# Turned placement for the inversion of two batches, and a new written order of all engines

## The chip, the cores and the metric

The kernel runs on one core of a Trainium2 chip. The metric is the device time of one execution in microseconds (us). The core's engines run side by side, each in the order of its own queue: TensorE (PE) multiplies matrices, VectorE (DVE), ScalarE (ACT) and GpSimd (POOL) work element by element, and SyncE (SP) issues the transfers (DMA). PE writes into PSUM, which has eight banks; the others read it there (not POOL) and keep their data in SBUF.

## The reference

Three stages, each fed by the one before. First a Nystrom attention for 4 batches of 8 heads, 576 positions and 64 features; then a layer with a cosine; then one with a leaky rectifier. q, k, v and alpha are float32, the weights of the layers 64-bit.

```
q_lm, k_lm = means over groups of 18 positions (32 landmarks)
A  = softmax(q k_lm^T / 8)      576 x 32
Bm = softmax(q_lm k_lm^T / 8)    32 x 32
C  = softmax(q_lm k^T / 8)       32 x 576
Z  = Bm^T / (norm1(Bm) * norminf(Bm) + 1e-6)
for 6 times:  Z = 2 Z - Z Bm Z
x  = A Z C v                          2304 x 512
h  = x w_in;  x = (h cos h) w_out     512 -> 2048 -> 512
h  = x w_in;  x = (max(h,0) + alpha min(h,0)) w_out
```

The iteration on Z is the inversion that the change is about: 32 matrices of 32x32, 8 in each batch.

## The kernel before, in words

**Storage and names.** A matrix product in full precision is made from rounded halves (high and low), three products for one. `acc`, `h` and `x` are rings of 4, 2 and 2 PSUM banks. All SBUF buffers lie in a few large tiles, so the profile shows nearly all of them as `m`.

**Units of work.** The code makes a list of operations, each with a name `unit:number`. `c` converts a block of 64-bit weights with three DVE steps (lines 575, 577, 579); `u0`, `u1` (batch 0) and `U2` to `U7` load q, k and v of half a batch, make landmarks, softmaxes and the products with v; `z0`, `z1`, `z2` are the inversions of batch 0, of batch 1, and of 2 and 3 together (`z_path`, line 888); `v` and `V` multiply the result with w_in of the first layer into V' (line 1059, casts at 1064 and 1066). `t0` to `t127` are ticks, a block of 128 hidden features for 288 positions: first product (1103), cosine on ACT and DVE (1108 to 1113), rounding (1115), subtraction for the low half (414, on POOL or DVE), second product into `acc` (1128). `b` are the blocks of the third stage, `s`, `y`, `o` and `x` units prepare its operands, `e` stores sums of the second. `w` are fillers (line 540): matmuls without a use, ten at the start and one behind each group of batch 0's inversion.

**Order.** Nothing is scheduled at run time. `ORDER` is one long list of the names; `Plan.go` issues the operations in that order, so each engine's queue is its part of the list. An operation that two engines can do goes to the first in its own list, or, with `/V`, `/A` or `/G` behind the name, to DVE, ACT or POOL. The engines wait for each other by semaphores.

**The inversion of batches 0 and 1 before.** Heads sit as 2 x 4: index i (2), and quadrant qd of 32 partitions (4). The operand of a head is Y = Z Bm (32 columns) beside Z C v (64 columns). A step (`mul`, line 958) multiplies, for each head, Y with both, 8 matmuls of 32x32 by 96, each in two instructions, from partitions of quadrant qd to partitions of the same quadrant of one bank. Then one DVE instruction (line 1006) makes 2 o - product. Five such steps, a last product for the 64 columns (line 1018 behind it), a product with Bm (`wm`, line 1025), and two copies of the result.

**The inversion of batches 2 and 3 before.** With 16 heads the step is another: `residue` (line 977, DVE) makes 2 I - Y once; then `turned` (line 985) multiplies with that, and sends heads of odd i to the neighbouring quadrant (qd xor 1) of a second bank; after six turns each is back. For each of the two banks DVE makes the next residue and ACT or DVE copies the product (`copy`, lines 409 and 411).

Of the kernel before, what the change touches and what calls it, by code (L numbers as in the profile page):

```python
# [13 lines left out]
ALU = mybir.AluOpType  # L14
# [6 lines left out]
u0:1 w:10 u0:2 w:4 c0:1 u1:1 w:2 w:3 u1:2 w:5 u0:4 c1:1 u0:18 c2:1 c9:1 u0:11 u0:5 u0:19 u1:3 c0:2 u0:6/V u0:7 u0:21/A  # L21
u0:20 w:7 c0:3 u0:12 u0:9 c0:4 u0:13 u1:18 u0:8 u0:10 u1:4 u0:22 c3:1 u1:19 u0:23 w:6 u1:20/A u0:3 c1:2 u1:21/A u0:14
c1:3 u1:9 u0:15 u1:7 c1:4 z0:1 u1:8 w:9 z0:2 u1:10 z0:3 c2:2 u0:24 c2:3 u1:5 c9:2 w:8 u0:25 u0:16 z0:4 u1:6 c2:4 w:1
U2:1 u0:17 c9:3 u1:22 u1:11 z0:5 u1:24 z0:6 z0:7 u0:26 z0:8 u0:28 u1:23 u1:12 u0:27 z0:9 c10:1 u1:16 u1:25 u1:13 u1:14
z0:10 c11:1 u1:26 u1:17 z0:11 u0:37 z0:12 u1:28 c9:4 U2:2 u1:27 c3:2 u1:15 u0:29 u0:38 u1:31 c3:3 u1:29 u0:30 u0:31
u0:39 u1:37 c4:1 u1:30 z0:13 u1:34 U3:1 z0:14 u1:32 u0:40 u0:32 u1:33 u0:34 u1:35 c3:4 u0:41 u0:33 u0:35 u1:36 u1:38
u1:39 c5:1 z0:17 u1:40 u0:42 w:11 U2:4 z0:15 u0:36 u1:41 z0:16 z0:18 u0:43 w:12 z0:20 c10:2 u1:42 w:13 z0:21 U2:5 u0:44
c10:3 z0:22 U2:6 u0:45 w:14 z0:23 u0:46 u1:43 z0:24 U2:13 z0:25 c11:2 z0:19 c10:4 z0:26 c11:3 c8:1 U2:14 z0:27 U3:2
u1:44 c11:4 z0:28 U2:16/A u1:45 c4:2 w:15 u1:46 z0:29 u0:47 z0:30 c6:1 w:16 z0:31 u0:48 c4:3 z0:32 U2:15/A u1:47 w:17
z0:33/A z0:34/A v0:1 u0:49/V u1:48 c4:4 v0:2 u1:49 c7:1 v0:4 v0:3 v0:5 U2:10 t0:1 c5:2 U2:12 U2:11 c5:3 U2:7 t0:2 U2:8  # L30
t0:3 t1:1 c8:2 c8:3 U3:13 c5:4 t0:4 c8:4 U3:14 t1:2 U2:9 c8:5 t1:3 c6:2 c12:1 t1:4 t0:5 U3:16/A U3:3 c6:3 U3:15/A t0:6
z1:1 c4:5 t1:5 t0:7 U2:19 z1:2 c5:5 z1:3 c4:6 U2:17 U2:32 t2:1 c2:5 U2:18 c5:6 c14:1 z1:4 U2:20 t1:6 t0:11 U2:21 U2:3
t2:2 U2:31 t0:8 U2:23 t2:3 t1:7 U2:22 t3:1 U2:33 c7:2 t0:10 z1:5 c6:4 v1:1 t2:4 z1:6 c7:3 c10:5 c6:5 t0:9 z1:7 c1:5 z1:8
v1:2 t1:8 t2:5 c6:6 c13:1 t1:11 v1:4 v1:3 t1:9 t2:6 v1:5 t1:10 t3:2 t2:7 t4:1 t3:3 z1:9 t3:4 c7:4 U2:24 t4:2 t3:5 c15:1
t2:8 U2:25 t4:3 t5:1 U2:26/V t4:4 z1:10 c12:2 t3:6 U3:4 t4:5 t5:2 U2:28 t3:7/V t4:6 t6:1 z1:11 c7:5 U2:29 t4:7 t5:3 U3:6
U3:5/V t2:9 c7:6 t6:2 t5:4 U3:7 t6:3 t5:5 t6:4 t2:11 c12:3 U3:8 t8:1 t6:5 U3:9 c14:2 t5:6 t7:1 c12:4 t8:2 t5:7 z1:12
c20:1 U3:10 t8:3 t2:10 t7:2 U3:12/V U3:11 U2:34 t7:3 t8:4 U2:27 z1:13 t6:6 t8:5 t7:4 U2:30 t6:7/V U3:17 t7:5 c14:3 U3:19
z1:14 U3:18 U2:35 t3:9 U3:20 t3:8 U3:21 U2:36 t3:11 U3:22 t3:10 U3:23 U3:31 c13:2 U3:24 z1:15 c13:3 t10:1 U3:25 U2:37
z1:16 U3:28 U3:32 U3:26 z1:17 c14:4 t10:2 U3:27 c13:4 c19:1 t9:1 U3:29 c3:5 c12:5 z1:18 U3:30 U2:38 c0:5 c13:5 c12:6/V
z1:20 c17:1 t9:2 U2:39 c14:5 z1:21 c9:5 t4:8 U3:33 t7:6 z1:22 c13:6 t4:10 z1:23 t10:3 t4:9 U2:40 z1:24 U3:34 t4:11 z1:25  # L40
# [36 lines left out]
U5:29 t50:4 t49:5 U4:35 t50:5 e47:6 e47:7 U6:14 U6:12 t47:8 U6:27 t49:6 t50:6 t49:7 t50:7 U6:13 U6:15 e47:2 U6:16 U5:24
# [272 lines left out]
def kernel(  # L350
# [537 lines left out]
    def z_path(bs, tz):  # L888
# [102 lines left out]
        if b == 2:  # L991
            residue(lambda o=o: o.t[:, :, 0:M], r=[o])
        for it in range(5):
            if b == 2:
                t, pps = zs(f"py{c}", [P, n, W]), [bank(c), bank(c)]
                turned(W, lambda o=o: o.t, [o], pps)
                for x, pp in enumerate(pps):
                    residue(lambda v_=half(pp, W): v_()[:, :, 0:M], slice(x, n, 2), [pp])
# [850 lines left out]
```

## Time and profile before

| | |
|---|---|
| median of the timed runs | 795.76 us (3 runs, 794.31 to 796.95) |
| the profiled execution | 791.91 us |
| its span, first to last instruction | 790.1 us |
| instructions | 18146 |
| PE, weight loads of PE, DVE, ACT, POOL busy | 775.1, 713.9, 637.6, 440.3, 247.5 us |
| granted TensorE clock, mean | 0.999 |

The table's busy times are sums over the span. The profile can cut them into stretches, name for each idle time what ended it, and list the instructions one by one; merged rows say `x` and a count. An instruction's source line can be that of a helper (414 is every subtraction, 409 and 411 every copy).

### The profile page before, as it was taken

The numbers are of one execution on the slowest core, as the hardware profiler recorded it, in microseconds if no ns is written. First come the engines' busy times: TensorE is split into PE (matmuls) and PEld (weight loads), VectorE is DVE, ScalarE is ACT, GpSimd is POOL, SyncE is SP. The second block draws the span as 40 slices with busy tenths as digits, with TensorE's granted clock in tenths as the row PEclk, the third lists the DMA queues.
The fourth block names the chain that finished last, engine by engine and source line by source line (L and its number), as shares of the span: only waits on it lengthen the run. The fifth ranks groups of instructions, "written<-read, shape, count | busy, mean of one in ns | idle before, by whom it ended". The sixth has DMA issues, their size and how long they took to land. (4 is left out here: it accounts for less than half of the span.)

```text
span 790.1 us, 18146 instructions
## 1 busy us (share of the span) xinstructions
PE 775.1 (98%) x6906; PEld 713.9 (90%) x6906; DVE 637.6 (81%) x1382; ACT 440.3 (56%) x998; POOL 247.5 (31%) x264
## 2 busy tenths in 40 slices
PE   9899999999999999999999999999999999999997
PEld 7577899998988999999998899889889999999997
DVE  5999988889888787886669797776978699776886
ACT  5497666778766555566755353233455475554431
POOL 0333232877522133535524442045311011000200
PEclk9999999999999999999999999999999999999999
DMA  9994457988967958765467863777166514563450
GB/s 294 258 277 135 124 162 161 201 200 184 280 196 243 308 167 264 231 213 170 156 213 270 280 205 118 257 244 256 50 214 223 215 47 144 189 204 122 131 199 28
DMA packets 114279, 154.81 MB, mean 196 GB/s; under 512 B 55568, under 2 KB 73488, under 8 KB 114192
## 3 DMA queue, kind: packets, MB, share of 16 engines
q1 hardware_dynamic: 114032, 153.39, 62.8%
q8 instruction: 54, 0.88, 0.5%
q14 instruction: 33, 0.27, 0.1%
q10 hardware_dynamic: 160, 0.26, 0.1%
HBM read 114.57 MB, written 39.06 MB: 194 GB/s over the span
## 5 line engine op out<-in xcount | busy, mean ns | idle before, releaser
L414 POOL TENSOR_TENSOR m<-m,m 128x288 fp32r<-128x288 f32 (+4 forms) x183 | 181.8, 1007 | 440.3 <-ACT m L1115 136.0
L1128 PE MATMUL acc<-m,m 128*128 128x288 f32 x1536 | 230.7, 297 | 0.0
L1128 PEld LDWEIGHTS acc<-m,m 128*128 128x128 f32 x1536 | 210.7, 188 | 14.6 <-issue 10.8
L414 DVE TENSOR_TENSOR m<-m,m 128x512 fp32r<-128x512 f32 (+5 forms) x261 | 145.6, 579 | 27.4 <-ACT m L1613 12.3
L1103 PE MATMUL h<-m,m 128*128 128x288 f32 x768 | 124.8, 299 | 0.6 <-DVE m L1113 0.4
L1103 PEld LDWEIGHTS h<-m,m 128*128 128x128 f32 x768 | 108.0, 188 | 7.0 <-DVE m L1113 4.0
L1778 PE MATMUL acc<-m,m 128*128 128x512 f32 x384 | 97.6, 392 | 0.0
L1112 ACT ACTIVATE m<-m,quarter 128x288 f32<-128x288 f32 x128 | 67.5, 534 | 39.7 <-DVE m L1110 39.0
L1509 PE MATMUL x<-m,m 128*128 128x256 f32 x588 | 84.8, 284 | 0.8 <-DVE m L414 0.6
L1778 PEld LDWEIGHTS acc<-m,m 128*128 128x128 f32 x384 | 68.2, 188 | 11.6
L1509 PEld LDWEIGHTS x<-m,m 128*128 128x128 f32 x588 | 75.5, 188 | 3.3 <-ACT m L409 1.0
L1113 DVE TENSOR_TENSOR m<-m,h 128x288 f32<-128x288 f32 x128 | 57.3, 450 | 25.6 <-ACT m L1112 19.9
L1613 ACT ACTIVATE m<-m 128x256 fp32r<-128x256 f32 (+2 forms) x96 | 45.8, 508 | 54.5 <-DVE m L1627 20.5
L1110 DVE SCALAR_TENSOR_TENSOR m<-h,m 128x288 f32<-128x288 f32 x128 | 57.3, 451 | 19.9 <-ACT m L1108 19.0
L1660 PE MATMUL acc<-m,m 128*128 128x256 f32 x485 | 70.0, 283 | 0.1
L1108 ACT ACTIVATE m<-h 128x288 int32<-128x288 f32 x128 | 51.7, 404 | 33.1 <-PE h L1103 31.4
L1115 ACT ACTIVATE m<-m 128x288 fp32r<-128x288 f32 x128 | 55.3, 439 | 26.1 <-DVE m L1113 21.7
L1660 PEld LDWEIGHTS acc<-m,m 128*128 128x128 f32 x485 | 63.2, 191 | 0.5 <-ACT m L1613 0.3
L409 ACT ACTIVATE m<-x 128x256 f32<-128x256 f32 (+6 forms) x80 | 31.1, 399 | 45.4 <-PE x L1509 28.5
L579 DVE SCALAR_TENSOR_TENSOR m<-m,m 128x512 int32<-128x512 int32 x64 | 46.8, 737 | 0.3
L577 DVE SCALAR_TENSOR_TENSOR m<-m,m 128x512 int32<-128x512 int32 x64 | 44.3, 697 | 0.4
L1465 PE MATMUL h<-m,m 128*128 128x256 f32 x300 | 42.7, 281 | 1.2 <-ACT m L409 1.2
(182 smaller groups left out, 1125.6 us busy)
## 6 DMA issues: line engine op xcount, KB each, us to landing
m<-wf2d SPq DMA_DIRECT2D x72, 512.0 KB, 5.0
m<-in_moe_w_in_dram SPq DMA_DIRECT2D x32, 512.0 KB, 6.0
m<-in_moe_w_out_dram SPq DMA_DIRECT2D x32, 512.0 KB, 5.9
wf2d<-m SPq DMA_DIRECT2D x28, 512.0 KB, 4.4
m<-w1d SPq DMA_DIRECT2D x32, 256.0 KB, 5.6
m<-wo2d SPq DMA_DIRECT2D x32, 256.0 KB, 3.2
y1d<-m SPq DMA_DIRECT2D x24, 288.0 KB, 5.0
m<-wi2d SPq DMA_DIRECT2D x20, 256.0 KB, 4.3
```

What stands on the lines that cost most here:

```text
L414: ENG[e].tensor_tensor(o, a, b, op=ALU.subtract)
L579: op(dve(512), lambda e: nc.vector.scalar_tensor_tensor(cf.t, rv(0), 29, cf.t, op0=ALU.logical_shift_right, op1=ALU.bitwise_or), r=[raw], ...
L1103: nc.tensor.matmul(out=hp.t[:, 0:CW], lhsT=w_[:, js], rhs=x[:, cs], start=(i == 0), stop=(i == 5))
L1108: op(act(CW, True), lambda e: nc.scalar.activation(k_.t, hp.t[:, 0:CW], AF.Copy, scale=INV2PI, bias=0.25), r=[hp], w=[k_], target=T + 0.8)
L1110: op(dve(CW), lambda e: nc.vector.scalar_tensor_tensor(u.t, hp.t[:, 0:CW], INV2PI, k_.t, op0=ALU.mult, op1=ALU.subtract), r=[hp, k_], w=[u])
L1112: op(act(CW), lambda e: nc.scalar.activation(u.t, u.t, AF.Sin, scale=2.0 * math.pi, bias=quarter), rw=[u], aset="sin")
L1113: op(dve(CW), lambda e: nc.vector.tensor_tensor(hc.t, u.t, hp.t[:, 0:CW], op=ALU.mult), r=[hp, u], w=[hc], target=T + 2.6)
L1115: op(act(CW), lambda e: nc.scalar.activation(gh.t, hc.t, AF.Copy), r=[hc], w=[gh, gl])
L1128: nc.tensor.matmul(out=yg[o].t[:, 0:CW], lhsT=w_.t[:, sl], rhs=x.t, start=(j == ja and i == 0), stop=(j == jb and i == 2),)
L1509: nc.tensor.matmul(out=rv(r), lhsT=a_.t[:, p, c2, js], rhs=b_.t[:, q_, c2], start=(first and c2 == 0 and y == 0), stop=(c2 == 1 and y == 2 ...
L1660: nc.tensor.matmul(out=yb.t[:, 256 * (p + yh):256 * (p + yh) + 256], lhsT=a_, rhs=b_, start=(st and p + yh + y == 0), stop=(en and y == 2) ...
L1778: nc.tensor.matmul(out=ya[n][t].t, lhsT=gv(x_), rhs=r_.t, start=(st and k == 0), stop=(en and k == 2))
```

## The change

Batches 0 and 1 get the step that batches 2 and 3 had: one residue, then five times a turned product into two banks (the second is the other bank name for batch 0, `h` and `x`, and a second `x` for batch 1), two residues and two copies, and a last turned product with two copies. `mul` stays for the first product. The filler behind each of batch 0's groups stays. An inversion of these has 51 operations in place of 34.

```
@@ z_path @@
-            op(("PE", 0.42), mm, r=[xb, *r], w=pps)
+            o1 = op(("PE", 0.105 * n), mm, r=[xb, *r], w=pps)
+            if not b:
+                filler(pps[0], 256, 1, [o1])
...
-        if b == 2:
-            residue(lambda o=o: o.t[:, :, 0:M], r=[o])
+        residue(lambda o=o: o.t[:, :, 0:M], r=[o])
         for it in range(5):
-            if b == 2:
-                t, pps = zs(f"py{c}", [P, n, W]), [bank(c), bank(c)]
...
-            t, pp = zs(f"py{c}", [P, n, W]), bank(c)
-            mul(lambda pp=pp: pp.t, W, lambda o=o: o.t[:, :, 0:M], lambda o=o: o.t, 0.42, [o], [pp])
-            vop(n * W, lambda e, o=o, t=t, v_=at_(pp, W): nv.scalar_tensor_tensor(
-                t.t, o.t, 2.0, v_(), op0=ALU.mult, op1=ALU.subtract), r=[o, pp], w=[t])
+            t, pps = zs(f"py{c}", [P, n, W]), [bank(c), bank(1 - c)]
+            turned(W, lambda o=o: o.t, [o], pps)
+            for x, pp in enumerate(pps):
+                residue(lambda v_=half(pp, W): v_()[:, :, 0:M], slice(x, n, 2), [pp])
+            for x, pp in enumerate(pps):
+                op([act(n // 2 * W, True), dve(n // 2 * W)], ... copy ...)
             o = t
```

The whole of `ORDER` is replaced, 4288 entries for 4254. Counted by engine: PE 1298 and SP 391 entries before and after; DVE 1372 before and 1425 after, ACT 967 and 970, POOL 226 and 204. Outside of `z0` and `z1`, 105 operations go from POOL to DVE and 83 from DVE to POOL, 57 from ACT to DVE and 39 from DVE to ACT. Cut to PE's queue from the start to the first V' product:

```
before: w:10 w:4 w:2 w:3 w:5 u0:18 u0:5 u0:19 u0:7 w:7 u0:12 u0:9 u1:18 u0:22 u1:19 w:6 u0:14 u1:9 u1:7 z0:1 w:9
        u0:24 u1:5 w:8 u0:16 w:1 u1:22 u1:24 u1:12 u1:16 u1:14 u0:37 u0:29 u1:31 u1:29 u0:31 u1:37 u1:33 u0:33
        z0:17 w:11 U2:4 w:12 z0:20 w:13 z0:22 w:14 z0:24 U2:13 z0:26 U2:14 z0:28 w:15 z0:30 w:16 z0:32 w:17 v0:1
after:  w:1 w:5 w:2 w:4 u0:18 u0:9 u0:19 u0:5 u0:7 w:7 w:9 w:8 u0:16 u0:24 u0:22 u1:7 u0:14 u1:5 u1:9 u1:19 u1:18
        w:6 u0:12 w:10 w:3 z0:1 u1:22 u1:24 u0:29 u1:12 u0:31 u0:37 u1:16 u1:29 u1:31 u1:14 w:11 z0:17 u0:33 u1:33
        u1:37 z0:21 w:14 U2:4 w:12 z0:26 z0:31 w:13 z0:36 U2:13 U2:14 z0:41 w:15 z0:46 w:16 z0:49 v0:1 w:17
```

In these, before, `z0:20` to `z0:28` are the five steps' products and `z0:30` the last one; after, they are `z0:21`, `26`, `31`, `36`, `41` and `46`. On DVE, ahead of the inversion's first reduction (`z0:2`) stand the steps of two conversions before and of four after. Up to the end of batch 0's inversion DVE gets the copies `u0:15`, `u0:17` (384 columns), `u0:21` and `u1:20` (128 columns), which ACT did, and one step of a conversion less. Of the copies in the new inversions one (`z0:47`) is on DVE in batch 0, and four (`z1:25`, `29`, `44`, `48`) in batch 1; the rest are on ACT. The loads change their order too: SP begins `u0:1 u0:2 c0:1 u1:1 u1:2 c1:1 c2:1 c9:1 u1:3` before and `u0:1 u0:2 c1:1 u1:1 c0:1 u1:2 c9:1 c2:1 c10:1 c3:1 u0:3 u1:3` after.

## Rows read from the trace of the kernel before

**Rows 1.** The page's part 1: busy time, share, instructions of each engine.
```profile
PE 775.1 (98%) x6906; PEld 713.9 (90%) x6906; DVE 637.6 (81%) x1382; ACT 440.3 (56%) x998; POOL 247.5 (31%) x264
```

**Rows 2.** Windows (us), length, then busy PE, PEld, DVE, ACT, POOL; clock, DMA share, GB/s.
```profile
0.00:20.00 20.00, 18.18 (x246) 14.60 (x247) 10.26 (x34) 11.07 (x21) 0.70 (x6) 1.00 0.93 293
20.00:40.00 20.00, 17.81 (x369) 11.72 (x368) 19.07 (x56) 9.66 (x27) 6.84 (x5) 1.00 1.07 258
40.00:60.00 20.00, 18.73 (x240) 15.80 (x239) 18.32 (x49) 18.63 (x41) 8.22 (x8) 1.00 0.98 278
60.00:80.00 20.00, 19.38 (x310) 15.11 (x309) 19.21 (x53) 13.37 (x30) 6.18 (x5) 1.00 0.38 124
80.00:240.00 160.00, 158.56 (x1711) 141.66 (x1710) 138.60 (x319) 110.87 (x261) 79.98 (x95) 1.00 0.76 191
...
400.00:600.00 200.00, 197.34 (x1285) 179.04 (x1284) 158.63 (x279) 86.14 (x191) 67.12 (x63) 1.00 0.62 212
...
780.00:791.00 11.00, 5.78 (x45) 5.18 (x43) 5.78 (x17) 1.58 (x5) 0.00 (x0) 0.89 0.17 49
```

**Rows 3.** Waits of PE: who waited for whom, us in total, times, longest.
```profile
PE x L730 <- DVE m L1066: 1.4, 1, 1.4
PE h L1465 <- ACT m L409: 1.2, 2, 1.0
```

**Rows 4.** Timeline, batch 0's inversion: start, length, engine, line, operation; idle before.
```profile
28.24 0.54 PE L961 MATMUL h<-m 32*32 32x96 f32 x16 [0.21 <-DVE m L971]
28.70 0.59 PE L540 MATMUL h<-m 128*128 128x192 f32 x2
29.09 0.35 DVE L1006 SCALAR_TENSOR_TENSOR m<-m,h 128x192 f32<-128x192 f32 x1
...
29.49 0.54 PE L961 MATMUL h<-m 32*32 32x96 f32 x16 [0.20 <-DVE m L1006]
```

**Rows 5.** Batches 2 and 3's inversion: timeline, and line 977 (ns min/median/max).
```profile
221.38 0.56 PE L985 MATMUL x<-m 32*32 32x96 f32 x32
...
221.87 1.07 PE L1103 MATMUL h<-m,m 128*128 128x288 f32 x6
...
227.12 0.33 ACT L409 ACTIVATE m<-x 128x192 f32<-128x192 f32 x1 [0.61 <-PE x L985]
...
L977 DVE TENSOR_TENSOR m<-m,x x10: 209/213/221, 220.4 to 229.9; 128x64 f32<-128x64 f32 x10
```

**Rows 6.** Windows of the inversions of batch 0 and batch 1.
```profile
25.86:36.92 11.06, 10.50 (x228) 7.68 (x222) 10.51 (x30) 3.85 (x9) 3.95 (x4) 1.00 1.07 284
69.20:83.00 13.80, 13.80 (x240) 10.64 (x238) 12.86 (x33) 7.34 (x16) 5.31 (x4) 1.00 0.54 171
```

**Rows 7.** Line 1006 in batch 1: count, ns min/median/max, first and last start.
```profile
L1006 DVE SCALAR_TENSOR_TENSOR m<-m,x x5: 347/356/356, 72.0 to 77.9; 128x192 f32<-128x192 f32 x5
```

**Rows 8.** Timeline of DVE at the start.
```profile
9.32 0.55 DVE L411 COPY m<-h 128x384 f32<-128x384 f32 x1
9.79 0.27 DVE L755 TENSOR_SCALAR m<-x 64x128 f32<-64x128 f32 x1
...
10.69 0.70 DVE L579 SCALAR_TENSOR_TENSOR m<-m,m 128x512 int32<-128x512 int32 x1
12.46 0.49 DVE L810 TENSOR_REDUCE m<-acc 128x1 f32<-128x320 f32 x1 [1.08 <-PE acc L793]
```

**Rows 9.** Groups by form, line 414 with 288 columns: count, busy, mean ns.
```profile
L414 DVE TENSOR_TENSOR m<-m,m 128x288 fp32r<-128x288 f32 x40 | 19.6, 491 | 3.8 <-ACT m L1115 3.7
L414 POOL TENSOR_TENSOR m<-m,m 128x288 fp32r<-128x288 f32 x88 | 75.7, 864 | 160.0 <-ACT m L1115 136.0 <-DVE m L1066 11.6 <-PE acc L1128 3.6
```

**Rows 10.** Timeline at the start of the third stage.
```profile
418.34 4.29 POOL L414 TENSOR_TENSOR m<-m,m 128x512 fp32r<-128x512 f32 x3 [14.00 <-ACT m L1251]
418.47 1.78 DVE L414 TENSOR_TENSOR m<-m,m 128x512 fp32r<-128x512 f32 x1
...
421.41 0.97 PE L1465 MATMUL h<-m,m 128*128 128x256 f32 x6 [0.99 <-ACT m L409]
```

More of the change, by code (lines that the diff above doesn't have):

```diff
@@ L26 @@
[L26 to L40, printed above, removed]
@@ L246 @@
[L246 to L247 removed]
+u0:1 u0:2 u0:4 w:1 w:5 w:2 w:4 c1:1 c1:2 u0:18 u1:1 u0:9 u0:19 u0:5 u0:7 w:7 u0:6/V u0:21 c1:3 u0:20 u0:10 c0:1 u0:11
+u0:8 w:9 w:8 u0:16 u0:24 u0:22 u0:17/V c0:2 c1:4 u1:4 u1:2 u1:7 u1:8 u0:14 u1:5 u1:9 c0:3 u0:25 c0:4 u0:23 u1:6 u1:10
+u1:19 u1:18 w:6 u0:15/V u0:26 u0:27 u1:21/A c9:1 u0:12 u0:13 u0:28 w:10 w:3 c2:1 u1:11 c9:2 c9:3 c9:4 c2:2 u1:20 z0:1
@@ new lines @@
+t111:10 t109:8 t110:8 t111:8 t113:4 t115:2 s64:23 t115:3 e111:5/V t113:5 t113:6 t114:6 t112:8 t116:1 e111:2/V e111:4/V
+t113:7/V t115:4 t116:2 t114:7/V t116:3 t115:5 y0:22 e95:6 y0:21 y0:2 t112:9 e111:1/V s64:24 s64:25 e111:3 t112:10
+t113:10 t114:10 t117:1 t115:6 y0:3 t112:11 t116:4 t116:5 t117:2 t117:3 t117:4 t115:7 y0:4 y0:5 t117:5 t113:8 t114:8
+t113:11 t119:1 t115:8 t118:1 t116:6 y0:16 y0:7 t119:2 t116:7/V t113:9 t116:8 y0:17 t114:9 y0:23 t119:3 y0:31 y0:11
+t118:2 t118:3 t114:11 t115:11 t115:9 y0:12 y0:6 y0:32 c57:5 s64:21 y0:24 y0:25 t118:4 t117:6 t119:4 t117:7/V t119:5
@@ L248 @@
+b37:22 b37:23 b38:23 b38:21 b37:24 b38:14 b39:11 b39:5 b39:6 b39:9 b39:10 b39:8 b39:12 b39:15 b39:16 b38:22 b38:20
+b39:19 b39:20 b39:21 b39:17 b39:13 b39:18 b39:26/V b39:14 b38:24 b39:22 b39:23 b39:27 b39:28 b39:29 b39:31 b39:30 b39:35
+b37:25 b38:25 b39:24 b39:32 b39:25 b39:33 b39:37 b39:34 b39:36
 """
@@ L993, in z_path @@
         for it in range(5):
-            if b == 2:
-                t, pps = zs(f"py{c}", [P, n, W]), [bank(c), bank(c)]
-                turned(W, lambda o=o: o.t, [o], pps)
-                for x, pp in enumerate(pps):
-                    residue(lambda v_=half(pp, W): v_()[:, :, 0:M], slice(x, n, 2), [pp])
-                for x, pp in enumerate(pps):
-                    op([act(n // 2 * W, True), dve(n // 2 * W)], lambda e, t=t, x=x, v_=half(pp, W), y0=M * (it == 4): copy(
-                        e, t.t[:, x:n:2, y0:W], v_()[:, :, y0:W]), r=[pp], w=[t])
-                o = t
-                continue
@@ L1004, in z_path @@
-            t, pp = zs(f"py{c}", [P, n, W]), bank(c)
-            mul(lambda pp=pp: pp.t, W, lambda o=o: o.t[:, :, 0:M], lambda o=o: o.t, 0.42, [o], [pp])
-            vop(n * W, lambda e, o=o, t=t, v_=at_(pp, W): nv.scalar_tensor_tensor(
-                t.t, o.t, 2.0, v_(), op0=ALU.mult, op1=ALU.subtract), r=[o, pp], w=[t])
-            o = t
-        pp, y = bank(c), zs("y6" + sx, [P, n, D])
-        if b == 2:
-            pps = [pp, bank(c)]
-            turned(D, lambda o=o: o.t[:, :, M:W], [o], pps)
-            for x, pp in enumerate(pps):
-                op([act(n // 2 * D, True), dve(n // 2 * D)], lambda e, x=x, v_=half(pp, D): copy(
-                    e, y.t[:, x:n:2], v_()), r=[pp], w=[y])
-        else:
-            mul(lambda pp=pp: pp.t, D, lambda o=o: o.t[:, :, 0:M], lambda o=o: o.t[:, :, M:W], 0.4, [o], [pp])
-            vop(n * D, lambda e, o=o, v_=at_(pp, D): nv.scalar_tensor_tensor(
-                y.t, o.t[:, :, M:W], 2.0, v_(), op0=ALU.mult, op1=ALU.subtract), r=[o, pp], w=[y])
+            t, pps = zs(f"py{c}", [P, n, W]), [bank(c), bank(1 - c)]
@@ new lines, in z_path @@
+            turned(W, lambda o=o: o.t, [o], pps)
+            for x, pp in enumerate(pps):
+                residue(lambda v_=half(pp, W): v_()[:, :, 0:M], slice(x, n, 2), [pp])
+            for x, pp in enumerate(pps):
+                op([act(n // 2 * W, True), dve(n // 2 * W)], lambda e, t=t, x=x, v_=half(pp, W), y0=M * (it == 4): copy(
+                    e, t.t[:, x:n:2, y0:W], v_()[:, :, y0:W]), r=[pp], w=[t])
+            o = t
+        pps, y = [bank(c), bank(1 - c)], zs("y6" + sx, [P, n, D])
@@ L1020, in z_path @@
+        turned(D, lambda o=o: o.t[:, :, M:W], [o], pps)
+        for x, pp in enumerate(pps):
+            op([act(n // 2 * D, True), dve(n // 2 * D)], lambda e, x=x, v_=half(pp, D): copy(
+                e, y.t[:, x:n:2], v_()), r=[pp], w=[y])
         pw = [bank(0), bank(1)]
```

432 lines of the change are left out of this document (220 added, 212 removed).

## The prediction

> **What bounds the kernel now.** I read the page's busy line first: TensorE (PE) is busy 775.1 us of a span of 790.1, so 15.0 us are all that any reordering could return unless PE's own work shrinks [rows 1]. The windows say where those 15 us lie: 2.2, 1.3 and 0.6 us in the three stretches of 20 us from 20 to 80, 1.4 from 80 to 240, 2.7 from 400 to 600, and the end, where 5.8 of the last 10.1 us are busy [rows 2]. What is left lies in the first 20 us (1.8), where the first matmul waits for constants and loads, and 0.7 in the other stretches. So there are two regimes. From 20 to 80 us VectorE (DVE) is as full as PE (19.1, 18.3 and 19.2 of 20) and the transfers are too until 60 (shares of 1.07 and 0.98). After that PE alone bounds, and an engine off its path only matters where PE is seen to wait. Third view, PE's waits: after the start the long ones are one of 1.4 us for a DVE cast of V', and two that add up to 1.2 for ScalarE (ACT) copies in the second block [rows 3].
>
> The profiled execution took 791.91 us (span 790.1 and 1.8 around it); the median of the timed runs is 795.76, 3.85 more. The sum below is made against 791.91, and 3.85 is added at the end.
>
> **The change, step by step.**
>
> *1. PE groups of the inversion.* One step of batch 0 or 1 is 8 matmuls of 32x32 by 96, 16 instructions. Before, head i of quadrant q writes to quadrant q, so both heads of a quadrant use the same square of the array. The group takes 0.54 us, and the next instruction starts 0.46 us after its start (28.24 and 28.70) [rows 4]. Batches 2 and 3 already run the turned placement, with 16 heads: 32 instructions in 0.56 us, the next one 0.49 us after the start [rows 5]. Twice the work in the same time: the two heads run side by side. Half that number of heads must then lie between 0.25 us (half of 0.49) and 0.49 (no gain, 0.03 more). I take 0.28, near the half, a little over it because the end of the last matmul does not halve. Twelve groups change (five steps and the last product, twice): 12 x 0.18 = 2.2 us of PE time, 1.1 in each batch.
>
> *2. Batch 1 (69 to 83 us).* PE is busy 13.80 of 13.80 us there [rows 6], and between the groups the order queues only ticks, which don't use the two x banks that a step now takes, so its saving is time: -1.1 (bounds -1.3, with 0.25, and +0.2, with 0.49).
>
> *3. What empties the banks.* A step lost one DVE instruction of 0.35 us [rows 7] and gets two residues and two copies. The nearest residue is 0.21 us (twice the width), the nearest copy 0.33 on ACT (twice the width) [rows 5]; I take 0.21 and 0.26. Per batch DVE loses 6 such instructions, 2.0 us, and gets 11 residues, 2.3 us, and those copies that the order gives it: one in batch 0, four in batch 1. That is +0.6 and +1.3 us on DVE. The other copies go to ACT, which is busy 3.85 of 11.06 and 7.34 of 13.80 us in these stretches [rows 6]: covered. DVE has only 0.55 and 0.94 us free there, so without spare room elsewhere the cost would be what is over that.
>
> *4. Batch 0 (25.86 to 36.92 us) and the start.* The chain there is: matmuls, DVE, matmuls. A step takes 1.25 us in the rows shown (28.24 to 29.49: 0.54 of matmuls, DVE from 29.09 to 29.44, 0.05 to the next) [rows 4]. The new step has 0.35 of matmuls, a residue, a second one behind it, and a copy beside them: 0.35 + 0.3 + 0.21 + 0.15 + 0.05 = 1.1. Over five steps, 0.7 less. Against this, DVE's order up to the last copy of this inversion gains four copies that ACT did (two of 0.55, two of 0.27) and loses one integer step of 0.70 [rows 8]: +0.9 and, with item 3, +1.5 us. DVE has holes ahead of it to take this in, one of 1.08 us at 11.4 [rows 8]; four weight conversions instead of two now stand ahead of the inversion's first reduction, which uses that hole if their loads have landed. Bounds: -1.5 (chain and PE saving) and +1.5 (DVE sets the pace). I take -0.5, nearer to the chain, as the hole is there in the row.
>
> *5. The seventh filler* is moved from ahead of the first V' product to behind it, into the wait of 1.4 us [rows 3]. A filler occupies PE for about 0.5. Bounds -0.5 and 0; I take -0.3.
>
> *6. The rest of the order.* PE's and SP's queues keep their entries (1298 and 391), in another order. From POOL to DVE go 105 entries and 83 the other way, from ACT to DVE 57 and 39 the other way: 40 more on DVE, at 0.49 us for the commonest form, against 0.86 on POOL [rows 9]. That is about +20 us on DVE's 638, and 20 fewer us on POOL. PE's path feels it only where PE waits. From 80 us to the end of the second-last window these waits come to about 4.8 us [rows 2]; the longest shown is at 420.41, behind a DVE subtraction that took 1.78 us beside one on POOL; PE started 0.99 late [rows 10]. An order drawn anew may remove or make such waits: bounds -3 and +3. I take -0.8, a sixth of what there is, because the work on PE after 80 us is the same and most of it has no wait to lose.
>
> *Sum:* -1.1 - 0.5 - 0.3 - 0.8 = -2.7. 791.91 - 2.7 = 789.2; with the 3.85 between profile and timed median, **793.0 us**. The likeliest case's own range is 791 to 795.
>
> **Rivals.**
>
> *Emptying the banks becomes the bound.* DVE is 10.51 of 11.06 us busy in batch 0's stretch and 12.86 of 13.80 in batch 1's [rows 6]; +1.5 and +1.3 us don't fit. Then batch 0 costs +1.5 and batch 1's PE saving is eaten (0), the rest 0: 791.91 + 1.5 + 3.85 = 797.3. For it: DVE's 19 of 20 us. Against it: residues and copies of half a group can start while the other half runs, and the holes at the start. The Trainium skill's page "TensorEngine Tiling (Array Packing)" (PSUM Bottleneck) says just this: tiling speeds up TensorE but not the emptying of PSUM, which may become the bottleneck, and both engines should share it. The trace so far agrees with half of it (DVE full, ACT with room).
>
> *Transfers.* The timed runs lie 3.85 us over the profile, with the same program; what differs between executions that is not in the instructions is when transfers land. If the new order of loads and their users takes half of it away: 789.2 + 1.9 = 791.1. For it: PE waits seldom for DMA in this profile, so the 3.85 must be waits not seen here. Against: nothing shows that they are DMA's.
>
> *DVE as the bound beyond the inversion (slower).* The place is 80 to 240 us, where DVE is busy 138.6 of 160 [rows 2], while PE has 1.4 us free. If a fifth of the 20 us that DVE gets arrives as PE waits (+4.0), and the start goes as in the first rival (+1.5, 0 for batch 1), it is 791.91 + 5.5 + 3.85 = 801.3. It decides from where DVE's results come later than the PE work queued ahead of their users; half that price gives 799.3. Against it: DVE's wait rows are for ACT and PE, and PE has several ticks queued ahead.
>
> *The turned placement gains nothing with 8 heads* (0.47 stays): items 2 and 4 give 0, the sum is -1.1: 794.7.
>
> **How the numbers follow.** A change under 0.3%, 2.4 us, can't be told from none here: faster is under 793.4, slower over 798.1. The forecast has 0.44, of which 0.29 lies under 793.4 (793.0 lies just inside it, and the bounds of item 6 are even) and 0.15 over; transfers 0.18 (faster); emptying 0.15 and no gain from placement 0.06 (no change); DVE beyond the inversion 0.17 (slower). That is 0.47 faster, 0.36 no change, 0.17 slower. The range for 8 in 10, 788.8 to 798.5, takes in the transfer case, with 2 us below it for item 6's bound, and the emptying case; what it leaves out, some 0.19, is most of the slower case and the far end of item 6.
>
> **What would show it.** Right: the turned groups of 16 instructions with the next start 0.25 to 0.3 us behind; batch 0's inversion under 10.6 us from its first product to the first V' product, and that product before 36.5; PE's wait on the V' cast about 1; PE busy about 773 with 14 to 15.5 us idle. Wrong: groups still at 0.46; the first V' product at 38 or later with DVE unbroken from 20 us; new PE waits on DVE from 80 us on; or a PE total that is the same, so that whatever moved the time were the waits. The forecast is wrong if the timed median is over 795 or under 791.

## The result, and the profile after

The changed kernel takes 801.26 us (median of 7 runs, 797.34 to 806.2), the kernel before in the same comparison 793.87 (7 runs, 791.23 to 796.95). The ratio is 1.0099, 95% interval 1.0076 to 1.0121: 1% slower, where the forecast was 793.0 and slower had a chance of 0.17. The profiled execution of the changed kernel took 803.73 us, 11.8 more than that of before; the medians differ by 7.4, so over a third of what the two profiles show is not typical.

Line numbers have moved: 414 is now 418, 409 is 413, 977 is 981, 985 is 989, 1059 is 1051, 1103 is 1095, 1564 is 1556, 1588 and 1591 are 1580 and 1583, 1660 is 1652, 1682 is 1674; each experiment's kernel has its own shift.

The busy line, the answer to [rows 1]: PE works 1.9 us more, not 2 less, and waits 24.9 us of its span in place of 15.0; DVE has 23 us more (some 20 had been foreseen).

```profile
PE 777.0 (97%) x6906; PEld 715.2 (89%) x6906; DVE 660.5 (82%) x1435; ACT 440.9 (55%) x1001; POOL 227.6 (28%) x242
```

The windows of the changed kernel, columns as in [rows 2], with two more stretches near the end:

```profile
0.00:20.00 20.00, 16.96 (x243) 14.03 (x243) 11.14 (x34) 10.23 (x17) 0.70 (x6) 1.00 0.86 289
20.00:40.00 20.00, 15.75 (x352) 10.86 (x351) 16.96 (x60) 10.22 (x32) 4.64 (x4) 1.00 0.87 216
40.00:60.00 20.00, 17.76 (x230) 13.56 (x229) 18.54 (x46) 16.67 (x34) 7.58 (x7) 1.00 0.77 218
60.00:80.00 20.00, 17.82 (x253) 14.31 (x252) 18.45 (x53) 15.88 (x37) 7.97 (x7) 1.00 0.57 176
80.00:240.00 160.00, 157.68 (x1739) 141.05 (x1745) 143.62 (x337) 110.94 (x263) 71.31 (x84) 1.00 0.76 190
400.00:600.00 200.00, 199.32 (x1305) 181.85 (x1304) 163.53 (x286) 87.07 (x190) 74.83 (x72) 1.00 0.59 205
740.00:764.00 24.00, 19.91 (x164) 19.50 (x164) 20.15 (x54) 6.63 (x16) 1.29 (x1) 1.00 0.48 145
764.00:768.00 4.00, 4.00 (x23) 4.00 (x22) 2.15 (x6) 1.67 (x4) 1.28 (x1) 0.57 0.67 225
```

The kernel before in the last two of these stretches:

```profile
740.00:764.00 24.00, 24.00 (x203) 24.00 (x202) 21.89 (x64) 6.43 (x17) 1.41 (x1) 1.00 0.60 194
764.00:768.00 4.00, 4.00 (x36) 4.00 (x35) 3.11 (x11) 1.86 (x5) 1.42 (x1) 1.00 0.06 25
```

Read stretch by stretch against [rows 2]: PE has lost 1.2, 2.1, 1.0 and 1.6 us in the first four, 0.9 from 80 to 240, and won 2.0 in 400 to 600. From 740 to 764, where PE before did not wait at all, it now waits 4.1 us; and in the 4 us after that it is "busy" throughout but gets 23 matmuls done in place of 36. The reason is the column after the busy times: its granted clock is 0.57 there, a mean of full speed and of half speed. At half speed for most of the 4 us PE loses about 0.43 x 4 = 1.7 us, and no idle column shows it. Waits and clock together are 5.8 us.

PE's longest waits in the changed kernel, grouped by who waited for whom (columns as in [rows 3]; left out is the one ahead of the first matmul):

```profile
PE h L1095 <- DVE m L1105: 2.5, 3, 1.2
PE x L1556 <- DVE m L1580: 2.3, 1, 2.3
PE h L847 <- DMA m<-in_v_dram: 2.2, 2, 1.2
PE x L1556 <- DVE m L1583: 1.7, 1, 1.7
...
PE h L989 <- ACT m L413: 1.4, 2, 0.9
```

The two of line 1556 are the stretch at 740. The timeline of PE and DVE there (merged rows carry a count):

```profile
748.68 1.59 PE L1556 MATMUL x<-m,m 128*128 128x256 f32 x12
752.01 0.98 PE L1556 MATMUL x<-m 128*128 128x256 f32 x6 [1.74 <-DVE m L1583]
...
762.49 1.73 PE L1556 MATMUL x<-m,m 128*128 128x256 f32 x12 [2.35 <-DVE m L1580]
764.02 0.83 PE L1652 MATMUL h<-m,m 128*128 128x256 f32 x3
```

```profile
749.49 0.75 DVE L1674 TENSOR_TENSOR m<-h,m 128x256 f32<-128x256 f32 x2
750.15 0.42 DVE L1674 TENSOR_TENSOR m<-acc,m 128x256 f32<-128x256 f32 x1
750.48 0.28 DVE L1619 TENSOR_TENSOR m<-m,m 128x128 f32<-128x128 f32 x1
750.68 0.42 DVE L418 TENSOR_TENSOR m<-m,m 128x256 fp32r<-128x256 f32 x1
751.01 0.48 DVE L1580 TENSOR_SCALAR m<-x,alpha_sb 128x256 f32<-128x256 f32 x1
751.53 0.42 DVE L1583 SCALAR_TENSOR_TENSOR m<-x,m 128x256 f32<-128x256 f32 x1
```

The reader is to see who waits for what. Line 1556 makes two products for one group of the third stage, one into each half of one `x` bank (`X.t[:, 256 * x:...]`), and DVE's lines 1580 and 1583 apply alpha to a half. PE has the first half done at 750.27 and its operands for the second half are there (in experiment 1 it does not wait). Yet it starts that half at 752.01, when DVE's 1583 has read the **first** half; and DVE comes to it only behind the instructions queued ahead, of which line 1674's are output work for another block. The kernel's own list of dependencies holds the halves apart (`w=[Xq[x]]`), the program as built does not: a write to a bank that stands in `ORDER` behind a read of that bank waits for the read. In the list of before, each of these second products stands ahead of the first half's reads; in the new one two stand behind them, `b33:2` and `b35:2`:

```
before:  b33:1 b33:2 b32:14 ... b31:45 b33:3 b33:5 b33:4
after:   b33:1 b32:17 s79:2 b32:16 b33:3 s79:3 b33:4 b33:7 b33:8 b33:2
before:  b35:2 b32:16 ... b34:8 b35:3
after:   b35:3 b33:18 s81:1 b32:22 b32:24 b35:2
```

b33:3 and b33:4 are lines 1580 and 1583 of that group, b35:3 is line 1580 of its own; the two waits are ended by just these lines. The queue of no engine is out of order: the fault is only in how the queues are interleaved. The Trainium skill, "Perfetto Trace Analysis" (Matmuls), has independent groups of matmuls rotate through different banks so that emptying one goes on beside the next; these two groups share one, and the trace shows the price, 1.74 and 2.35 us.

### The profile page after: what moved, and what is told of

The parts are those of the page before. It is cut to its first block, busy times and chain, and to the rows that moved or that the text cites. A ratio compares the mean times of both kernels' runs of the same rounds, so it can differ in the third digit from the quotient of the medians.

```text
span 801.9 us, 18173 instructions
## 1 busy us (share of the span) xinstructions
PE 777.0 (97%) x6906; PEld 715.2 (89%) x6906; DVE 660.5 (82%) x1435; ACT 440.9 (55%) x1001; POOL 227.6 (28%) x242
## 4 chain that ended last, share of the span: by engine, by line
PE 74%; DVE 11%; DMA 7%; ACT 4%; issue 2%; SPq 1%; POOL 1%; DVEq 0%; ACTq 0%; POOLq 0%
PE acc L1120 20%; PE acc L1770 11%; PE h L1095 10%; PE x L1501 9%; PE acc L1652 6%; PE h L1457 5%; PE x L1457 4%; PE h L1652 3%; DVE m L418 2%; DMA m<-in_moe_w_in_dram 2%; PE x L1556 2%; PE x L1051 2%; PE x L1652 1%; DMA m<-wi2d 1%; DVE m L581 1%
## 5 line engine op out<-in xcount | busy, mean ns | idle before, releaser
L418 POOL TENSOR_TENSOR m<-m,m 128x288 fp32r<-128x288 f32 (+4 forms) x164 | 167.5, 1036 | 448.5 <-ACT m L1107 160.8
L418 DVE TENSOR_TENSOR m<-m,m 128x512 fp32r<-128x512 f32 (+5 forms) x280 | 160.6, 595 | 26.9 <-ACT m L1605 9.1
L1605 ACT ACTIVATE m<-m 128x512 fp32r<-128x512 f32 (+2 forms) x96 | 46.6, 510 | 52.6 <-DVE m L1619 21.1
L1100 ACT ACTIVATE m<-h 128x288 int32<-128x288 f32 x128 | 51.9, 405 | 26.2 <-PE h L1095 24.9
L413 ACT ACTIVATE m<-x 128x256 f32<-128x256 f32 (+7 forms) x96 | 33.7, 365 | 52.0 <-PE x L1501 29.1
L581 DVE SCALAR_TENSOR_TENSOR m<-m,m 128x512 int32<-128x512 int32 x64 | 48.1, 754 | 0.3
L583 DVE SCALAR_TENSOR_TENSOR m<-m,m 128x512 int32<-128x512 int32 x64 | 45.7, 721 | 0.4
```

What stands on the lines that cost most here:

```text
L418: ENG[e].tensor_tensor(o, a, b, op=ALU.subtract)
L581: op(dve(512), lambda e: nc.vector.scalar_tensor_tensor(cf.t, rv(1), -0x40000000, cf.t, op0=ALU.bitwise_and, op1=ALU.bitwise_or), r=[raw], ...
```

## The experiments

Each median stands beside that of the kernel before in the same comparison (794.0 to 795.0).

**1. The tail repaired.** Two places of the list put back; every queue as in the changed kernel.

```
- b33:3 s79:3 b33:4 b33:7 b33:8 b33:2      - b35:3 b33:18 s81:1 b32:22 b32:24 b35:2
+ b33:2 b33:3 s79:3 b33:4 b33:7 b33:8      + b32:22 b32:24 b35:2 b35:3 b33:18 s81:1
```

> The changed kernel with two places of the end of its order put back: the second-half product of two groups of the last stage (b33:2 and b35:2) stands again ahead of the DVE read of the first half of the same bank (b33:3, b35:3); nothing else moves, and every engine's own queue is the same. Theory: the two waits of PE on DVE at 750.27 (1.74 us) and 760.14 (2.35 us) in the changed kernel are there because PE's write of the second half waits for that read, which is queued behind other DVE work; and the granted clock of 0.50 and 0.65 between 764 and 768 follows from these waits. Then both waits and the low clock go: 4.1 us of waits and about 1.7 us of clock, the time falls from 801.3 to 794 to 797, PE idles under 0.5 us between 745 and 765, and the mean granted clock of all timed runs is 0.999. Rival 1: DVE is simply late there, and the next PE instruction in the queue waits instead: the time stays within 1 us of 801.3. Rival 2: the waits go but the clock falls anyway at the end: 797 to 799.

Measured 795.16 (12 runs), before 794.96; ratio 1.0009 (0.9991 to 1.0026). That is 6.1 us under the changed kernel, and the 0.2 us that are left over the kernel before can't be told from no change. Windows of this run:

```profile
740.00:764.00 24.00, 24.00 (x202) 23.82 (x201) 21.89 (x65) 8.50 (x21) 2.79 (x2) 1.00 0.56 178
764.00:768.00 4.00, 4.00 (x36) 4.00 (x35) 2.39 (x7) 0.51 (x2) 0.00 (x0) 1.00 0.15 30
```

No wait, the full clock, 36 matmuls. The mean granted clock of its runs is 0.997 to 1.000; in the changed kernel's runs 0.992 to 0.999.

**2. The same fault put into the kernel before.** The reads moved ahead of b33:2 and b35:2 in the old list, with all queues as before.

```
- b33:2 b32:14 b32:20 b34:1 ... b31:45 b33:3        (PE's b33:2 ahead of DVE's b33:3)
+ b32:14 b32:15 b32:7 b31:44 b31:50 b32:8 b31:45 b33:3 b33:2 b32:20 b34:1 ...
  (b35:2 and b35:3 likewise)
```

> The kernel before with the same two products (b33:2, b35:2) put behind the DVE read of the other half of their bank, as in the changed kernel; every engine's own queue is the same as in the kernel before. It does that part of the change alone. Theory: PE waits at both places for a read that is queued behind other DVE work, 1 to 3 us each, with a lower granted clock in some of the runs after it: 795.0 + 3 to 7 = 798 to 802. Rival: in the old order DVE is early enough there: under 796, with no PE wait over 0.5 us between 740 and 770.

802.07 (6 runs), before 794.54; 1.0104 (1.0074 to 1.0134). The kernel before with this alone is as slow as the changed kernel. PE's waits from 740 to 770 us, and two windows, one within the longer wait and one from its end on:

```profile
PE x L1569 <- DVE m L1593: 5.7, 2, 4.1
```

```profile
757.00:761.00 4.00, 0.10 (x1) 0.00 (x0) 3.28 (x11) 1.10 (x3) 0.00 (x0) 0.97 0.69 218
761.00:765.00 4.00, 3.79 (x20) 3.79 (x21) 1.18 (x5) 0.25 (x1) 0.00 (x0) 0.60 0.00 1
```

5.7 of waits and 0.40 x 4 = 1.6 of clock make 7.3; measured were 7.5. The two waits are 1.6 and 4.1 us here, 1.74 and 2.35 in the changed kernel, as other DVE work stands ahead of the reads: the run shows the mechanism, and a cost of the same order, not the same cost.

**3. One of the two repaired.**

```
- b35:3 b33:18 s81:1 b32:22 b32:24 b35:2          (b33:2 stays behind b33:4)
+ b32:22 b32:24 b35:2 b35:3 b33:18 s81:1
```

> The changed kernel with only the second of the two products (b35:2) put back; the first wait (1.74 us at 750.27 in the changed kernel) stays. Theory: the low clock needs the second wait behind the first. Then the first costs its own 1.7 us only, the mean granted clock is 0.999, and the time is 795.2 + 1.7 = 796.9, within 796 to 798. Rival: one wait of 1.7 us is enough for the low clock: 798 to 800, with a stretch of a granted clock under 0.9 between 750 and 770.

797.78 (9 runs), before 794.54; 1.0059 (1.0037 to 1.0080), 2.6 us over experiment 1 for a wait of 1.73. In its profile the clock stays at 1.00; but of its nine runs six have a mean clock of 0.998 or less and take 797.75 to 800.66, and three 0.999 or more and take 795.68 to 796.69. So with one wait of 1.7 us the low clock seems to come in some executions and in some not; where in the slower ones it fell is not shown, as only the first of the nine has a trace. The time lies in the theory's range, but the theory's clock of 0.999 holds for three runs only.

**4. The old inversion in the new order**, with the faulty tail, **and 5. the same with the tail repaired.**

```
-            turned(W, ...); residue x 2; copy x 2          (each step, batches 0 and 1)
+            mul(W, ...); 2 o - product                     (where the later residue stood)
```

> The changed kernel's order with the inversion of batches 0 and 1 as before (one bank, one DVE instruction per step), which stands where the later of the two residues stood. It undoes the placement alone. Theory A (the order is what costs): the time stays at 800 to 803, with the waits for the load of v at 24.5 and 26.9 us and the two waits near 750 and 760 all there. Theory B (the placement costs): it falls by 3 us or more, under 798.5.

> The changed kernel's order with the inversion of batches 0 and 1 as before and with the two products b33:2 and b35:2 put back ahead of the DVE read of the other half of their bank. So of the change only the order is left, without those two waits. Theory (the two costs add: the two waits with the low clock behind them about 6 us, the split inversion about 2 to 3): the time is 799.1 - 6.1 = 793.0, within 792 to 794, that is 1 to 3 us under the kernel before and 1.5 to 3 under the run with the tail repaired (795.2). Rival: the split inversion costs nothing by itself in this order, and the run with the old inversion was faster only through the lower number of low-clock stretches: the time is that of the repaired tail, 795.2 within 0.8.

With the fault 799.09 (9 runs; 1.0064, 1.0042 to 1.0086), without it 795.25 (12 runs, before 794.54; 1.0017, 0.9995 to 1.0038). The waits for v, which theory A expected in the first, are not in its profile. Both waits of the tail are, but with the full clock behind them:

```profile
PE x L1569 <- DVE m L1593: 2.3, 1, 2.3
PE x L1569 <- DVE m L1596: 1.7, 1, 1.7
```

```profile
764.00:768.00 4.00, 4.00 (x36) 4.00 (x35) 2.45 (x8) 0.72 (x2) 0.00 (x0) 1.00 0.34 130
```

Five of its nine runs are at 798.0 to 799.1 with a mean clock of 0.999, the other four at 801.0 to 803.3 with 0.997 or less. The changed kernel's runs lie alike: 797.3 and 799.8 at 0.999, 800.7 and 801.3 at 0.997 (its profiled one, 803.7 at 0.998, has the waits for v besides). So its gain of 2.2 us over the changed kernel, which I would have put down to the placement, goes with the clock; and against the repaired tail (795.16) no gain of the old inversion can be seen (795.25; each is known to some 1.5 us). My expectation of 793.0 for the sum was wrong, its rival right.

**6. The new inversion in the old order.**

```
- z0:20 w:13 z0:21 ...                      (product, 2 o - product)
+ z0:21 w:13 z0:22 z0:25 z0:23 z0:24 ...    (product, residue, copy of the other bank, residue, copy)
```

> The kernel before with the inversion of batches 0 and 1 as changed (odd heads turned into a second bank, two residues on DVE and two copies on ACT per step), put into the old order of all engines; U2:4 to U2:6 stand ahead of z0:17 and the products U2:13 to U2:16 where the two banks allow it. It does the placement alone. Theory A (the order of the rest is what costs, the placement itself gains): PE's groups save 0.14 us each, 1.7 in all, and the time is 791.5 to 793.9, at or under the kernel before (793.9). Theory B (the placement itself costs, since a step now ends with a residue on DVE and behind it a copy on ACT from the same bank): one step of batch 0 is longer than the 1.25 us of before, batch 0 ends 1.5 us later and batch 1 3 us later, and the time is 796 to 799.

798.34 (12 runs), before 794.96; 1.0041 (1.0024 to 1.0057): theory B's time. Its mechanism is only in part what is seen. The first residue of batch 1, its wait, and the stretch behind it:

```profile
72.97 1.18 DVE L983 TENSOR_TENSOR m<-m 128x64 f32<-128x64 f32 x1
```

```profile
74.30 0.40 PE L991 MATMUL x<-m 32*32 32x96 f32 x16 [1.67 <-DVE m L983]
```

```profile
75.00:79.00 4.00, 4.00 (x46) 2.97 (x45) 2.78 (x9) 1.61 (x8) 1.47 (x2) 0.57 0.80 288
```

One instruction of 0.2 us took 1.18, beside a GpSimd multiplication (72.41 to 74.08); PE waited 1.67 for it, and then lost some 1.7 by the clock. Those 3.4 us are the largest part of what this execution loses. They are not all of it: the first V' product stands at 38.08, 1.2 us behind the 36.92 of before. Of these, 0.8 are there ahead of batch 0's first turned product (29.00 against 28.24), and 0.4 come from the steps: 8.2 us from that product to `wm` (at 37.20) against 7.8 (28.24 to 36.04). The theory had said 1.5 for batch 0.

**7. The loads of v earlier.**

```
- c10:1 c10:2 ... c3:1 u0:3 u1:3
+ u0:3 u1:3 c10:1 c10:2 ... c3:1
```

> The changed kernel with the eight loads of v for batches 0 and 1 (u0:3, u1:3 on SP) moved ahead of the loads of two weight tiles (c10:1, c3:1), which they followed; nothing else moves. Before the change the last of them was issued at 17.2 us, after it at 22.4. Theory: PE's waits of 1.24 and 0.93 us for v at 24.50 and 26.93 go, batch 0's first inversion product moves forward by about 2 us, and the first V' product stands at 37.5 to 38.2 instead of 39.9; the time falls by 1.5 to 2.5, to about 799. Rival 1: the chain of batch 0 is then held by DVE, whose conversions of the two weight tiles now wait for their later loads: the first V' product stays after 39 and the time within 0.7 of 801.3. Rival 2: what is gained at 38 us is lost again at the next late DVE result before 240: under 0.7 as well, but with the first V' product before 38.5.

803.83 (4 runs; 1.0104, 1.0074 to 1.0134): no faster than the changed kernel. The waits for v went, and a longer one came, because the weight tile now landed late and DVE's queue held up everything behind its conversion. DVE's row, PE's wait, and the window behind:

```profile
23.14 0.43 DVE L582 TENSOR_SCALAR m<-m 128x512 int32<-128x512 int32 x1 [3.57 <-DMA m<-in_moe_w_in_dram]
```

```profile
PE h L832 <- ACT m L824: 3.2, 1, 3.2
```

```profile
24.00:32.00 8.00, 6.22 (x120) 5.00 (x122) 5.91 (x28) 3.42 (x10) 1.16 (x1) 0.57 1.07 259
```

This is the first rival, and harder than it was put: the first V' product stands at 42.60 us.

**8. Residues and copies crossed**, on the repaired tail.

```
- z0:25 z0:24 z0:23 z0:22   ...   z0:28 z0:27 z0:29 z0:30   ...
+ z0:22 z0:25 z0:23 z0:24   ...   z0:27 z0:30 z0:28 z0:29   ...
```

> The kernel with the tail repaired, in which the four instructions that empty the two banks of a step of the inversions of batches 0 and 1 follow each other as: residue of the first bank, copy of the second, residue of the second, copy of the first (in the changed kernel's order both copies stand ahead of both residues in some steps and behind them in others). Their engines and all else are unchanged. Theory: residue (DVE) and copy (ACT) of the same bank run one after the other in the order in which they stand, and a step's length comes from that series; crossed, the two engines work on different banks, PE's waits for the ACT copies in batch 0 (0.94 and 0.44 us in the run with the tail repaired) shrink to under 0.7 together, and the time falls by 0.7 to 1.5, to 793.7 to 794.5. Rival: DVE's other work that stands between is what holds a step, not the series: the waits only change places, the time stays at 795.2 within 0.6.

798.57 (10 runs), before 794.54; 1.0054 (1.0034 to 1.0074): 3.4 slower than the repaired tail, against both. PE's waits for the copies of batch 0 are 1.8 us where they were 1.4. In this execution the clock fell behind them, with no single wait over 0.8 us ahead of it:

```profile
37.00:45.00 8.00, 7.25 (x48) 5.03 (x42) 6.45 (x13) 3.79 (x10) 1.71 (x1) 0.57 0.99 271
```

Why it fell here and not in experiment 1, whose waits in that stretch are as long, stays open. Nor is the clock the whole cost: five of the ten runs have a mean clock of 0.999 or more, and their median is still 798.24. In batch 1 the crossing makes a new wait:

```profile
78.00 1.28 ACT L1107 ACT_TABLE_LOAD   x1
...
79.73 0.23 ACT L416 ACTIVATE m<-x 128x96 f32<-128x96 f32 x1
...
80.00 0.19 DVE L984 TENSOR_TENSOR m<-m,x 128x32 f32<-128x32 f32 x1 [2.08 <-ACT m L416]
...
80.50 0.40 PE L992 MATMUL x<-m 32*32 32x96 f32 x16 [1.22 <-DVE m L418]
```

By changing places the copy on ACT has moved back in ACT's queue too, behind a load of an activation table (in experiment 1 it runs at 75.35, ahead of that load at 76.47). The residue of its bank, and with it all of DVE, waits 2.08 us for this copy. So the edit did more than cross the readers, and its 3.4 us are not the price of the crossing alone.

**9. A slow conversion put behind a tick**, on the repaired tail.

```
- z1:12 c12:3 t5:4 t5:5
+ z1:12 t5:4 t5:5 c12:3
```

> The changed kernel with the tail repaired and one DVE instruction, the third step of a weight conversion (c12:3), put behind a tick's subtraction (t5:5) instead of ahead of it. In the run with the tail repaired that conversion took 1.72 us at 59.60 (0.68 where GpSimd does not work at the same time), and PE waited 1.07 us at 60.66 for the subtraction behind it. Theory: that wait goes and nothing takes its place: 795.2 - 1.0 = 794.2, within 793.5 to 794.7. Rival: the slow instruction only moves, the next product waits for it instead: 795.2 within 0.5, with a PE wait of 0.5 us or more somewhere between 60 and 64.

794.78 (12 runs), before 794.57; 1.0015 (0.9996 to 1.0033): not to be told from experiment 1. PE's wait of 1.07 us is gone, and one of 0.68 us stands instead before its next product in `h` (at 64.34, behind DVE's line 1108): the rival.

**10 to 12. The old order for the start, the new one, repaired, for the rest**, with the old inversion, meeting at 220, 243 and 121 us.

```
- ORDER = old
+ ORDER = old[:n], w:17 behind v0:1, then the repaired new one without what is done     (n = 1300, 1480, 700)
```

> The kernel before as far as about 220 us (the first 1300 entries of its order, with the seventh filler behind the first V' product as in the changed kernel), and from there on the changed kernel's order with the two products of the tail put back; the inversion of batches 0 and 1 as before. Theory (PE's waits add up, whichever order they come from): up to there the kernel before has 1 to 2 us less of PE waits than the changed order, and behind it the changed order has about 1.3 us less (1.9 against 3.2 in the profiles): 794.5 - 1.3 - 0.2 for the filler = 793.0, within 792 to 794. Rival: the place where the two orders meet makes waits of its own of 1 us or more near 220 us: 794 to 796.

> As the run of two orders before, but they meet at about 243 us (entry 1480 of the old order), behind the inversion of batches 2 and 3: the kernel before with the seventh filler behind the first V' product up to there, and from there on the changed order with the two products of the tail put back. The run that met at 220 us had one PE wait of 2.23 us at 220.97 at the meeting place and then 6.83 us at half clock; without both its span would be 797.5 - 2.2 - 3.4 = 791.9. Theory (the meeting place alone was wrong): no PE wait over 0.6 us between 215 and 260, the clock at 1.00, and the time 791.9 + 1.8 = 793.7, within 793 to 794.6, the same as or a little under the kernel before. Rival: the changed order behind an old start is itself slower (what it finds done at 240 us is not what it was drawn for): over 795.5 with waits spread over 240 to 600.

> The same with the meeting place at about 121 us (entry 700): the old order and the old inversion for the start, the changed order with the repaired tail for all the rest. Theory: what the changed order lost before its tail was repaired lies at the tail alone, and what differs from 121 to 740 us is a wash: 794.6 within 1, and no low clock before the end. Rival: the middle of the changed order is better by 0.3% or more by itself: under 792.5. Second rival: a wait of over 1.5 us at the meeting place and a low clock behind it: 797 or more.

At 220: 799.91 (6 runs; 1.0073, 1.0050 to 1.0095). The meeting place, within the inversion of batches 2 and 3, made one wait (its rival, whose 794 to 796 is passed), and the clock more than doubled it. PE's row and the window:

```profile
223.20 0.89 PE L990 MATMUL x<-m 32*32 32x96 f32 x32 [2.23 <-DVE m L982]
```

```profile
222.00:230.00 8.00, 6.80 (x106) 5.75 (x114) 4.88 (x14) 4.61 (x10) 0.90 (x1) 0.57 0.27 55
```

2.2 + 0.43 x 8 = 5.6; measured were 5.3. At 243: 795.52 (12 runs; 1.0018, 0.9997 to 1.0038); the meeting place is clean there, but a wait of 1.71 us at 194.9, in the old part, had not been foreseen, and the time is 0.9 over the theory's range; it touches the rival's 795.5, but no waits are spread over 240 to 600 (one of 1.0 us). At 121: 793.55 (12 runs), before 794.00; 0.998 (0.9956 to 1.0003): the lowest of all, but not to be told from the kernel before. So no version here beats it for sure.

## Why the prediction was wrong

**The step that failed is item 6**, the rest of the order: "the work on PE after 80 us is the same and most of it has no wait to lose". True of the old waits: the third stage did win 2.0 us (197.34 to 199.32). But an order can also make waits where there were none, and half clock behind them: 5.8 us at 750 to 768, outside the bounds of 3 up and down. The bounds were taken from the waits that the trace had, not from what in the new list could wait, and the clock was put at nothing without a reason. Among the prediction's signs of being wrong stood "new PE waits on DVE from 80 us on"; these two are such waits. The diff shows it: a write of a bank behind a read of the same bank. Experiments 1 and 2 take the fault out and put it in: -6.1 and +7.5.

**The sum without that** would have been 791.9 - 1.9 + 3.85, and measured is the kernel before plus 0.2 (-0.7 to 2.1, by the interval). So items 2 to 5 did not gain their 1.9 either, though the third stage's 2.0 are in it:

*Item 1* was right in kind and mis-sized. The group and the next instruction in batch 1 of the changed kernel:

```profile
76.38 0.40 PE L989 MATMUL x<-m 32*32 32x96 f32 x16
...
76.70 0.67 PE L1120 MATMUL acc<-m,m 128*128 128x288 f32 x3
```

The next start is 0.32 to 0.33 behind, not 0.28: of 0.46 it saves 0.14, twelve times some 1.7 us, not 2.2. Half the heads do not take half the time.

*Items 2 and 4.* Of the 1.7 us less of PE work, waits take back 1.2: with the repaired tail batch 0's products wait 0.94 and 0.44 us for ACT copies, and one of batch 1 waits 0.28, where the old inversion in the same order (experiment 5) waits 0.48 once in batch 0. The chain gets a link, which I had put "beside" the residue: a copy (ACT) of a bank starts when the residue (DVE) of it has ended, or the other way round, in the order of the list. In batch 1:

```profile
77.08 0.27 DVE L981 TENSOR_TENSOR m<-m,x 128x32 f32<-128x32 f32 x2
...
77.35 0.25 ACT L413 ACTIVATE m<-x 128x96 f32<-128x96 f32 x1 [0.38 <-DVE m L981]
...
77.66 0.40 PE L989 MATMUL x<-m 32*32 32x96 f32 x16 [0.28 <-ACT m L413]
```

The first V' product stood at 39.88 us in the changed kernel, where I had named 36.5 as the limit; 2.2 us of it are the waits for v. In experiment 1's execution, with the same queues, there were none, and it stood at 37.73: still 0.8 behind the 36.92 of before. With the old inversion in the same order (experiment 5) it stood at 37.64: nearly all of the 0.8 is the order, and the turned steps gain nothing there.

*Item 3* was right: a residue takes 0.18 us (0.21 taken), a copy 0.25 (0.26).

```profile
L981 DVE TENSOR_TENSOR m<-m,x x10: 172/180/184, 77.1 to 86.6; 128x32 f32<-128x32 f32 x10
```

*Item 5:* PE's wait on the V' cast is 0.88 in place of 1.42, but 0.33 has appeared ahead of the V' product, where the filler had been: -0.2 (taken -0.3).

*The rivals.* The slower one came out by its number (801.3) and not by its mechanism, so that hit is luck: from 80 to 240 us DVE got 5 us more [rows 2] and PE lost 0.9. No rival had a wait in the last stage, or the clock. The rival on transfers took it that only the landing of transfers differs between executions; that is not so, as the mean clock of the 26 runs of the kernel before beside experiment 1 goes from 0.996 to 1.000. It does not explain the spread either: those at 1.000 take 790.8 to 796.6, and what spreads them stays open.

## What to carry to other kernels

When an order is drawn anew, don't bound its effect by the waits of the old one: go through the new list for each write of a buffer or bank that stands behind a read of the same, though of another part, and ask what is queued ahead of that read on its engine. In this kernel, where PE fills 98% of the span, a wait on it of some 2 us could cost twice its length, as the clock behind it was lower; so read the granted clock beside the idle columns, and compare single runs of the same mean clock. And a change that takes instructions from one engine but puts one more hand-over into a chain should be priced by the chain.

## What the runs showed of the hardware

**The clock.** The same in five profiles: with PE waits of 1.67, 1.85, 2.23, 2.35, 3.25 and 4.11 us the granted clock fell to its lower level (0.50 from 764 to 766 us in the changed kernel: 1.2 of 2.4 GHz) for a few us, already during the wait or up to 1.5 us behind it; in a sixth (experiment 8) among small matmuls with waits of at most 0.78. With single waits of 1.71 and 1.73 us, and twice with the pair of 1.73 and 2.34 (experiments 4 and 7), it stayed up. The Trainium skill, "TensorE: Matmul & The Clock Gate" (Part 1), says that the low clock is the default and activity releases it; the traces agree in kind: it falls with waits, though not with every one, and where the work ends (0.89 over the last window of [rows 2]). Its price, estimated as the lost share of the clock times the length of the windows above, is 1.6 to 3.4 us each time.

**DVE beside GpSimd.** The conversion step that takes 0.69 us alone (at 76.73 in the same run) took 1.72 when it started within a GpSimd subtraction, and with it held up a tick (experiment 1's kernel):

```profile
59.60 1.72 DVE L584 SCALAR_TENSOR_TENSOR m<-m,m 128x512 int32<-128x512 int32 x1
```

```profile
59.49 1.28 POOL L421 TENSOR_TENSOR m<-m,m 128x512 fp32r<-128x512 f32 x1 [1.79 <-ACT m L566]
```

Residues of 0.2 us became 1.18 (experiment 6) and 1.08 (the run that met at 220 us, at 221.97, beside 221.75 to 222.91 on GpSimd), each time at the head of a chain on which PE then waited. The Trainium skill, "SBUF — State Buffer", tells of a port pair that DVE and GpSimd share, held for a whole instruction by whichever comes first; on DVE's side it names instructions with two inputs in SBUF, as these are. These rows agree.
